# A fused layernorm, state-space and SwiGLU kernel: the half-width matmuls of all four chunks gathered in one stretch, one layernorm and four gate/up tiles moved forward

## The chip, the cores and the metric

One Trainium2 chip, one of its cores. The metric is the device time of one execution in microseconds (us); lower is better. The core works through five instruction queues, each in order: TensorE (PE, matmuls; its weight loads are shown apart as PEld), VectorE (DVE), ScalarE (ACT), GpSimd (POOL) and SyncE (SP, which only issues DMA transfers). They meet at semaphores.

## What is computed

```python
x  = A_x                                    # 1 x 2048 x 512, bf16
xn = layernorm(x)                           # over the 512 columns, eps 1e-5
# branch A: a diagonal complex recurrence along the 2048 rows
Bu[t] = xn[t] @ B_bar.T                     # complex, 512 states
h[t]  = Lam_bar * h[t-1] + Bu[t]
A = 2 * real(h @ C.T) + xn * Dskip
# branch B: SwiGLU, hidden width F = 1376
B = (silu(xn @ w_gate) * (xn @ w_up)) @ w_down
out = x + A + B
```

## The kernel before, in words

The 2048 rows are cut into four **chunks** of 512 (`CW`), c = 0 to 3, and each chunk into four row tiles of 128. Everything that a matmul reads of `xn` is its transpose `xnT`, so each chunk passes through these stages:

- **Layernorm** (`ln_rest`, L583). On DVE, for each row tile, `ln_stats` (L182: L183 and L184); then one small add (L198). POOL raises to the power -0.5 (L199), DVE forms the bias `nb` (L202), ACT writes the normalised tile `xn` (`norm_act`, L212), and SP issues a DMA transpose of it into `xnT` (L227). `ln_rest` gives two lists: the statistics (with the power), and a tail, which is `nb` and then four times "normalise one tile and transpose it". Chunk 0 has its own code at the head, and chunk 1 normalises on DVE (L207); chunks 2 and 3 do it on ACT. The buffer `xn` is single.
- **Input product of the recurrence** (`bproj_chunk`, L661): eight PSUM banks of four 128x512 matmuls (L352), copied to `u16` by ACT (L354).
- **The recurrence on DVE** (`ssm_ops`): a rotation of six wide operations (L362, L372, L376), eight scans (L394), six tiny operations that form the carry for the next chunk (L403 to L408), and a rotation back into `wt`.
- **Gate and up** (`gateup_chunk`, L669): F = 1376 is ten tiles of 128 columns and a last one of 96. A full tile is eight matmuls (L427) in two banks; ACT takes the silu of one (L441) and copies the other (L442), DVE multiplies two tiles at once (L446). The last tile (`gateup_last`, L450) packs its 96 gate columns and 32 of its 96 up columns in one bank (L453). The other 64 up columns come from `wu_last`; they fill only half of the array's columns, so two chunks share a bank, one in each half: for chunks 0 and 1 this is done when chunk 1 comes to its last tile, for chunks 2 and 3 at chunk 3's (eight matmuls each, L463). ACT copies them out (L466), and DVE multiplies (L468).
- **Output** (`out_chunk`, L675): four banks, one for each row tile, are filled by eleven matmuls from the gate/up product (L514), stay open, and are completed by eight matmuls from the recurrence (L524, which read `wt` and the matrix `CF`, made by `c_ops` from DVE L338 and ACT L335). ACT copies them out (L530) and POOL issues DMA transfers that add them to the output in memory, where `x` was copied before (L735). The last chunk goes through DVE L527.

The **order of every queue** is the order in which the program writes instructions out. PE's order is written by hand, stage after stage: gate/up of chunk 0, with its `bproj` inside; `bproj_chunk(1)`; `gateup_chunk(1)`; `bproj_chunk(2)`; `out_chunk(0)`; `gateup_chunk(2)`; `bproj_chunk(3)`; `out_chunk(1)`; `gateup_chunk(3)`; `out_chunk(2)`; `out_chunk(3)` (L725 to L753). Gate/up takes the last tile of a chunk first (L670).

The work of DVE, and of ACT and SP where an operation of the list contains it, waits in a list, `backlog`. `queue(tag, ops)` puts operations with a cost behind it, and `spread` alternates between two lists. After each piece of PE work `pump(us)` adds its time to what is owed, and writes out operations from the front as long as half of the first one's cost is owed. `need(tag)` writes out all that stands in front of the last operation with that tag. `multiply(keep)` writes out the gate/up products. Before the change, chunk 2's layernorm stands in chunk 0's recurrence and chunk 3's in chunk 1's.

PSUM is one pool of eight banks. A matmul that starts in a bank waits until ACT has copied out what was in it.

Of the kernel before, what the change touches and what calls it, by code (L numbers as in the profile page):

```python
# [11 lines left out]
BF16 = mybir.dt.bfloat16  # L12
ALU = mybir.AluOpType
# [10 lines left out]
def kernel(  # L24
# [17 lines left out]
    nc = tc.nc  # L42
    _, L, D = A_x.shape
# [3 lines left out]
    CW = 512  # L47
    HW = CW // 2
    NT = L // 128
    NCH = L // CW  # L50
    TPC = CW // 128
    KD = D // 128
    NQ = Pst // 128
    FT = (F + 127) // 128
# [4 lines left out]
    LA, LB = 32, 64  # L59
# [8 lines left out]
    up_p = ctx.enter_context(tc.tile_pool(name="up_p", bufs=4))  # L68
# [5 lines left out]
    def bank(shape=(128, CW), dtype=F32):  # L74
        return psum.tile(list(shape), dtype, name="ps")
# [11 lines left out]
    xnT = const.tile([128, KD, L], BF16, name="xnT")  # L87
# [8 lines left out]
    wu_last = const.tile([128, KD, LB], BF16, name="wu_last")  # L96
# [85 lines left out]
    def ln_stats(n):  # L182
        nc.vector.bn_stats(out=stats[:, n, 0, :], in_=xall[:, n, :])  # L183
        nc.vector.bn_aggr(out=mv[:, n, :], in_=stats[:, n, 0, :])  # L184
# [12 lines left out]
    def ln_rstd(a, b):  # L197
        nc.vector.tensor_scalar(out=ve[:, a:b], in0=mv[:, a:b, 1], scalar1=EPS, scalar2=None, op0=ALU.add)  # L198
        nc.gpsimd.tensor_tensor(out=rstd[:, a:b], in0=ve[:, a:b], in1=neg_half[:, 0:b - a], op=ALU.pow)  # L199

    def ln_nb(a, b):
        nc.vector.scalar_tensor_tensor(out=nb[:, a:b], in0=mv[:, a:b, 0], scalar=-1.0, in1=rstd[:, a:b],  # L202
                                       op0=ALU.mult, op1=ALU.mult)
# [21 lines left out]
    def xT_dma(n):  # L225
        c, i = divmod(n, TPC)
        nc.sync.dma_start_transpose(out=xnT[:, :, n * 128:(n + 1) * 128], in_=xn_tile(c)[:, i, :])  # L227
# [12 lines left out]
    V = nc.vector  # L240
# [106 lines left out]
    def bproj_tile(c, part, q):  # L347
        if c not in u_tiles:
            u_tiles[c] = ssm.tile([128, 2, NQ, CW], BF16, name="u16", bufs=2)
        ps = bank()  # L350
        for k in range(KD):
            nc.tensor.matmul(ps[:], lhsT=BT[:, part, k, q * 128:(q + 1) * 128], rhs=xnT[:, k, c * CW:(c + 1) * CW],  # L352
                             start=(k == 0), stop=(k == KD - 1))
        nc.scalar.copy(out=u_tiles[c][:, part, q, :], in_=ps[:])  # L354
# [65 lines left out]
    gu_tiles = {}  # L420
    u_pair = {}
    products = []
# [7 lines left out]
    def gu_tile(c):  # L430
        if c not in gu_tiles:
            gu_tiles[c] = gut.tile([128, FT, CW], BF16, name="guT")
        return gu_tiles[c]
# [14 lines left out]
    up_last = {}  # L448

    def gateup_last(c):  # L450
        ps = bank()
        for k in range(KD):
            nc.tensor.matmul(ps[:], lhsT=w_last[:, k, :], rhs=xnT[:, k, c * CW:(c + 1) * CW],  # L453
                             start=(k == 0), stop=(k == KD - 1))
        u = up_last[c] = up_p.tile([128, CW], BF16, name="ul", bufs=2)
        nc.scalar.activation(out=gu_tile(c)[0:LB + LA, FT - 1, :], in_=ps[0:LB + LA], func=ACT.Silu)
        nc.scalar.copy(out=u[LB:LB + LA, :], in_=ps[LB + LA:128])
        if c % 2 == 0:
            return
        ps = bank()  # L460
        for k in range(KD):
            for i in range(2):
                nc.tensor.matmul(ps[i * LB:(i + 1) * LB], lhsT=wu_last[:, k, :],  # L463
                                 rhs=xnT[:, k, (c - 1 + i) * CW:(c + i) * CW], start=(k == 0), stop=(k == KD - 1))
        for i in range(2):
            nc.scalar.copy(out=up_last[c - 1 + i][0:LB, :], in_=ps[i * LB:(i + 1) * LB])  # L466
            g, u = gu_tiles[c - 1 + i][0:LB + LA, FT - 1, :], up_last[c - 1 + i][0:LB + LA, :]
            products.append(lambda g=g, u=u: V.tensor_tensor(out=g, in0=g, in1=u, op=ALU.mult))  # L468

    def gateup_tile(c, fi):  # L470
        if fi == FT - 1:
            return gateup_last(c)
        psg = bank()
        gu_mm(psg, wg_g, c, fi, 0, CW)
        psu = bank()
        gu_mm(psu, wu_g, c, fi, 0, CW)
        gu_out(c, fi, psg, psu)
# [29 lines left out]
    def out_ffn(n):  # L507
        c, i = divmod(n, TPC)
        o_tiles[n] = []
        for lo, hi in out_blocks(n):  # L510
            o = bank((128, hi - lo))
            o_tiles[n].append(o)
            for fi in range(FT):
                nc.tensor.matmul(o[:], lhsT=gu_tiles[c][:fsz[fi], fi, i * 128:(i + 1) * 128],  # L514
                                 rhs=wd_sb[:fsz[fi], fi, lo:hi], start=(fi == 0), stop=False)
# [23 lines left out]
    def queue(tag, ops, at=None):  # L539
        ops = [[op[0], op[1], op[2] if len(op) > 2 else None, tag] for op in ops]  # L540
        if at is None:
            backlog.extend(ops)
        else:
            backlog[at:at] = ops

    def step():
        for item in backlog[0:AHEAD + 1]:
            if item[2] is not None:
                item[2]()
                item[2] = None  # L550
        cost, op, _, _ = backlog.pop(0)
        op()
        owed[0] -= cost

    def pump(us):

        owed[0] += us
        while backlog and owed[0] >= backlog[0][0] * 0.5:
            step()
        if not backlog:  # L560
            owed[0] = 0.0

    def multiply(keep):

        while len(products) > keep:
            products.pop(0)()
            owed[0] -= 0.65

    def need(tag):

        while any(item[3] == tag for item in backlog):
            step()
# [10 lines left out]
    def ln_rest(c, on_act):  # L583
        ops = [(0.7, lambda n=n: ln_stats(n)) for n in range(c * TPC, (c + 1) * TPC)]
        def fin():
            ln_rstd(c * TPC, (c + 1) * TPC)
        def nbf():
            ln_nb(c * TPC, (c + 1) * TPC)
        ops += [(0.1, fin)]
        tail = [(0.1, nbf)]  # L590
        for n in range(c * TPC, (c + 1) * TPC):
            def one(n=n):
                (norm_act if on_act else norm_dve)(n)
                xT_dma(n)
            tail.append((0.05 if on_act else 0.35, one))
        return ops, tail
# [64 lines left out]
    def bproj_chunk(c):  # L661
        need(f"ln{c}")
        for part in range(2):
            for q in range(NQ):
                bproj_tile(c, part, q)
                pump(BP)
                multiply(0 if q else 1)

    def gateup_chunk(c):  # L669
        for fi in [FT - 1, *range(FT - 1)]:  # L670
            gateup_tile(c, fi)
            pump(GU)
            multiply(1)

    def out_chunk(c):  # L675

        multiply(0)
        for n in range(c * TPC, (c + 1) * TPC):
            out_ffn(n)
            pump(FT * 0.2163)  # L680
        need(f"ssm{c}")
        need("cf")
        for n in range(c * TPC, (c + 1) * TPC):
            out_ssm(n)
            pump(2 * NQ * 0.2163)

    def spread(ops, others, tag, tag2):

        others = list(others)
        for op in ops:  # L690
            queue(tag, [op])
            if others:
                queue(tag2, [others.pop(0)])

    def queue_ssm(c):
        fwd, back = ssm_ops(c)
        queue(f"ssm{c}", fwd + back)
# [10 lines left out]
            multiply(0 if q else 1)  # L708
    fwd0, back0 = ssm_ops(0)
    stats2, norm2 = ln_rest(2, True)  # L710
    queue("ssm0", fwd0[0:2] + [(1.5, params_b)] + fwd0[2:6])
    queue("ln2", stats2)
    queue("ssm0", fwd0[6:8])
    spread(fwd0[8:] + back0, norm2, "ssm0", "ln2")
    queue("cf", c_ops())
    load_late()
    for fi in range(G0, FT):
# [6 lines left out]

    bproj_chunk(1)  # L725
    fwd1, back1 = ssm_ops(1)
    stats3, norm3 = ln_rest(3, True)
    queue("ssm1", fwd1[0:6])
    queue("ln3", stats3)
    queue("ssm1", fwd1[6:8])  # L730
    spread(fwd1[8:] + back1, norm3, "ssm1", "ln3")
    gateup_chunk(1)
    nc.gpsimd.dma_start(out=dsk_bc[:], in_=A_Dskip.partition_broadcast(128))
    bproj_chunk(2)
    nc.sync.dma_start(out=out[0, 0:(NT - TPC) * 128, :], in_=A_x[0, 0:(NT - TPC) * 128, :])  # L735
    queue_ssm(2)
    out_chunk(0)
    gateup_chunk(2)
    bproj_chunk(3)
    fwd3, back3 = ssm_ops(3)  # L740
    queue("ssm3", fwd3)
    for n in range(0, NT - TPC):
        queue("skip", [skip_op(n, False)])
        if n % TPC == TPC - 1:
            queue("skip", [(0.0, lambda c=n // TPC: skip_store(c))])
    queue("ssm3", back3)
    out_chunk(1)
    gateup_chunk(3)
    for n in range(NT - TPC, NT):
        queue("skip", [skip_op(n, True)])  # L750
    out_chunk(2)
    need("skip")
    out_chunk(3)  # L753
# [30 lines left out]
```

## Time and profile before

| | |
|---|---|
| time of three runs | 180.7, 181.02, 181.13 us (median 181.02) |
| the profiled execution's own time | 181.21 us |
| its span, first to last instruction | 179.4 us |
| PE busy | 173.4 us, 97% |
| DVE busy | 155.0 us, 86% |
| ACT busy | 104.8 us, 58% |
| start of `bproj_chunk(2)` on PE | 59.27 us |
| start of the first scan of chunk 0 on DVE | 45.84 us |

Times inside the profile count from the start of the span. The profile has a page of sums, a chain of work that ended last (followed back from the last instruction to what released it), a timeline by engine, a list of waits, and a table by stretches of time with the granted clock of TensorE. In a timeline a row is: start, duration, engine, line, operation, output and input, and how many such instructions are merged in it; in brackets, how long the engine sat idle before it and what ended that. Matmuls are pipelined: one of 512 columns is listed with 379 ns, but in a dense row they start 216 ns apart.

### The profile page before, as it was taken

To read this page: it belongs to the slowest core of one execution; us is meant where nothing else is said; L and a number is where in the kernel's file an instruction comes from. 1 tells how busy PE (TensorE), PEld (TensorE's weight loads), DVE (VectorE), ACT (ScalarE), POOL (GpSimd) and SP (SyncE) were. 2 spreads that over 40 slices of the span, in tenths; PEclk is the share of its full clock that TensorE was granted. 3 is DMA by queue.
4 is the path that set the end of the run, shared out by engine and by line. 5 is a ranking of instruction groups with operands and counts; after the bars stand their busy time and mean duration, and the time that the engine had idled before them with its cause. 6 is when DMAs were issued, how large, how long until landed. Compare 5 with 4: busy or idle time off the path is not lost.

```text
span 179.4 us, 2491 instructions
## 1 busy us (share of the span) xinstructions
PE 173.4 (97%) x908; PEld 83.4 (46%) x924; DVE 155.0 (86%) x248; ACT 104.8 (58%) x190; POOL 23.4 (13%) x30
## 2 busy tenths in 40 slices
PE   7899999999999999999999999999999999999993
PEld 2684444443444444444444444444444444444742
DVE  3649998799999999999999999999999986996033
ACT  3459956998299959022799661024866949805000
POOL 7001100000500000025400000014000004315000
PEclk9999999999999999999999999999999999999999
DMA  5999757994036600011840000007300007964512
GB/s 147 294 263 210 163 98 177 357 190 109 5 72 168 252 4 0 0 11 22 112 93 2 0 0 4 0 0 80 37 0 5 0 0 109 139 103 45 76 58 61
DMA packets 28492, 15.53 MB, mean 87 GB/s; under 512 B 18336, under 2 KB 28416, under 8 KB 28448
## 3 DMA queue, kind: packets, MB, share of 16 engines
q1 hardware_dynamic: 24592, 11.87, 28.5%
q0 software_dynamic: 3456, 3.28, 14.4%
q10 hardware_dynamic: 432, 0.23, 0.4%
q8 instruction: 7, 0.11, 0.3%
q14 instruction: 5, 0.04, 0.1%
HBM read 8.03 MB, written 5.24 MB: 74 GB/s over the span
## 4 chain that ended last, share of the span: by engine, by line
PE 93%; DMA 2%; SPq 1%; DVE 1%; issue 1%
PE ps L427 36%; PE ps L514 21%; PE ps L352 15%; PE ps L524 15%; DMA xall<-in_A_x_dram 2%; PE ps L609 2%; PE ps L453 2%; PE ps L463 1%; SPq L118 1%; DVE stats L183 0%; PE ps L219 0%; SPq L126 0%; SPq L120 0%; DVE xn L207 0%; DVE xall L527 0%
## 5 line engine op out<-in xcount | busy, mean ns | idle before, releaser
L514 PE MATMUL ps<-wd_sb,guT 128*128 128x512 bf16 (+4 forms) x195 | 38.6, 355 | 0.2
L427 PE MATMUL ps<-xnT,wg 128*128 128x512 bf16 x143 | 37.6, 379 | 0.3
L427 PE MATMUL ps<-xnT,wu 128*128 128x512 bf16 x146 | 37.5, 379 | 0.1
L394 DVE TENSOR_TENSOR_SCAN g<-r_t,car,u 128x512 bf16<-128x512 f32 x24 | 28.9, 1263 | 0.0
L524 PE MATMUL ps<-CF,wt 128*128 128x512 bf16 (+2 forms) x140 | 28.1, 355 | 0.2
L352 PE MATMUL ps<-xnT,BT 128*128 128x512 bf16 x126 | 28.2, 379 | 0.1
L514 PEld LDWEIGHTS <-guT 128*128 128x128 bf16 (+1 forms) x198 | 18.5, 98 | 19.9
L441 ACT ACTIVATE guT<-ps 128x512 bf16<-128x512 f32 x40 | 25.2, 629 | 2.5 <-PE ps L427 2.3
L442 ACT CAST u<-ps 128x512 bf16<-128x512 f32 x40 | 24.7, 618 | 2.7 <-PE ps L427 2.7
L427 PEld LDWEIGHTS <-wu 128*128 128x128 bf16 x148 | 14.5, 98 | 17.5
L427 PEld LDWEIGHTS <-wg 128*128 128x128 bf16 x148 | 14.3, 98 | 17.6 <-issue 0.8
L530 ACT CAST res<-ps 128x512 bf16<-128x512 f32 x12 | 6.8, 582 | 23.5 <-PE ps L524 23.5
L524 PEld LDWEIGHTS <-wt 128*128 128x128 bf16 x144 | 13.4, 98 | 14.3
L531 POOL DMA_DIRECT2D out_dram<-res x12 | 10.5, 1033 | 72.6 <-ACT res L530 67.5
L352 PEld LDWEIGHTS <-BT 128*128 128x128 bf16 x128 | 12.5, 98 | 15.1
L354 ACT CAST u<-ps 128x512 bf16<-128x512 f32 x32 | 17.7, 614 | 2.4 <-PE ps L352 2.2
L486 ACT ACTIVATE xr<-xall,nb,rstd 128x512 bf16<-128x512 bf16 x16 | 12.0, 808 | 8.4 <-DVE xall L492 5.9
L183 DVE BATCH_NORM_STATS2 stats<-xall 128x6 f32<-128x512 bf16 x16 | 10.7, 671 | 3.2 <-DMA xall<-in_A_x_dram 3.2
L446 DVE TENSOR_TENSOR guT<-guT,u 128x1024 bf16<-128x1024 bf16 x20 | 13.5, 679 | 0.0
L527 DVE TENSOR_TENSOR xall<-ps,xall 128x512 bf16<-128x512 f32 (+2 forms) x6 | 3.1, 514 | 9.1 <-PE ps L524 9.1
L199 POOL TENSOR_TENSOR rstd<-ve,neg_half 128x4 f32<-128x4 f32 x3 | 5.3, 1751 | 43.6 <-DVE ve L198 43.6
L362 DVE TENSOR_TENSOR pm<-u,c 128x2048 bf16<-128x2048 bf16 x8 | 9.8, 1221 | 1.2 <-ACT c L279 1.1
(101 smaller groups left out, 169.0 us busy)
## 6 DMA issues: line engine op xcount, KB each, us to landing
out_dram<-in_A_x_dram SPq DMA_DIRECT2D x1, 1536.0 KB, 8.7
out_dram<-res POOLq DMA_DIRECT2D x12, 128.0 KB, 3.2
out_dram<-xall POOLq DMA_DIRECT2D x3, 512.0 KB, 5.7
wd_sb<-in_B_w_down_dram SPq DMA_DIRECT2D x1, 1280.0 KB, 10.1
xall<-in_A_x_dram SPq DMA_DIRECT2D x1, 1024.0 KB, 5.9
wg<-in_B_w_gate_dram SPq DMA_DIRECT2D x1, 512.0 KB, 6.1
wu<-in_B_w_up_dram SPq DMA_DIRECT2D x1, 512.0 KB, 7.1
xall<-in_A_x_dram SPq DMA_DIRECT2D x1, 512.0 KB, 7.9
```

Source lines behind the costliest of these rows:

```text
L183: nc.vector.bn_stats(out=stats[:, n, 0, :], in_=xall[:, n, :])
L352: nc.tensor.matmul(ps[:], lhsT=BT[:, part, k, q * 128:(q + 1) * 128], rhs=xnT[:, k, c * CW:(c + 1) * CW], start=(k == 0), stop=(k == KD - 1))
L354: nc.scalar.copy(out=u_tiles[c][:, part, q, :], in_=ps[:])
L394: V.tensor_tensor_scan(out=g()[:, part, q, :], data0=r_t[:, q:q + 1].to_broadcast([128, CW]), data1=u_tiles[c][:, part, q, :], initial=ini ...
L427: nc.tensor.matmul(ps[:fs, lo:hi], lhsT=wslice(groups, fi, k), rhs=xnT[:, k, c * CW + lo:c * CW + hi], start=(k == 0), stop=(k == KD - 1))
L441: nc.scalar.activation(out=guT[:fs, fi, :], in_=psg[:fs], func=ACT.Silu)
L442: nc.scalar.copy(out=u_pair[c][:fs, fi % 2, :], in_=psu[:fs])
L446: products.append(lambda: V.tensor_tensor(out=g, in0=g, in1=u, op=ALU.mult))
L486: nc.scalar.activation(out=box["xr"][:], in_=xall[:, n, :], func=ACT.Identity, scale=rstd[:, n:n + 1], bias=nb[:, n:n + 1])
L514: nc.tensor.matmul(o[:], lhsT=gu_tiles[c][:fsz[fi], fi, i * 128:(i + 1) * 128], rhs=wd_sb[:fsz[fi], fi, lo:hi], start=(fi == 0), stop=False)
L524: nc.tensor.matmul(o[:], lhsT=w_tiles[c][:, part, q, i * 128:(i + 1) * 128], rhs=CF[:, part, q, lo:hi], start=False, stop=(part == 1 and q ...
L531: nc.gpsimd.dma_start(out=out_v[:, n, lo:hi], in_=res[:, lo:hi], accum_op=ALU.add)
```

## The change

Four things are done.

1. The half-width matmuls of all four chunks stand together, in a new function `up_halves`, between `gateup_chunk(1)` and `bproj_chunk(2)`: eight for chunks 0 and 1, then eight for chunks 2 and 3. The copies by ACT follow, and the last-tile products of chunks 0 and 1 are queued there; chunks 2 and 3 queue theirs in `gateup_last`. The buffers `ul` are four in place of two.
2. So that `xnT` of chunk 3 is there, its layernorm is moved from chunk 1's recurrence into chunk 0's, behind chunk 2's: on DVE, six scans of chunk 0 come before chunk 3's statistics, then two scans and the carry, then chunk 3's `nb`, and the four pairs of normalisation and transpose alternate with the rotation back. `need("ln2")` and `need("ln3")` stand in front of `up_halves`.
3. Chunk 2's tiles 0 to 3 of gate and up are computed inside `out_chunk(0)`, between the two groups of its matmuls.
4. Chunk 2's last tile comes at the end of its gate/up stage, as number 10 of `range(4, FT)`.

```diff
-        u = up_last[c] = up_p.tile([128, CW], BF16, name="ul", bufs=2)
+        u = last_up(c)
         nc.scalar.activation(out=gu_tile(c)[0:LB + LA, FT - 1, :], in_=ps[0:LB + LA], func=ACT.Silu)
         nc.scalar.copy(out=u[LB:LB + LA, :], in_=ps[LB + LA:128])
-        if c % 2 == 0:
-            return
-        ps = bank()
-        for k in range(KD):
+        if c >= 2:
+            last_product(c)
+
+    def last_up(c):
+        if c not in up_last:
+            up_last[c] = up_p.tile([128, CW], BF16, name="ul", bufs=NCH)
+        return up_last[c]
+
+    def last_product(c):
+        g, u = gu_tiles[c][0:LB + LA, FT - 1, :], last_up(c)[0:LB + LA, :]
+        products.append(lambda: V.tensor_tensor(out=g, in0=g, in1=u, op=ALU.mult))
+
+    def up_halves():
+        pair = [bank() for _ in range(0, NCH, 2)]
+        for c0, ps in zip(range(0, NCH, 2), pair):
+            for k in range(KD):
+                for i in range(2):
+                    nc.tensor.matmul(ps[i * LB:(i + 1) * LB], lhsT=wu_last[:, k, :],
+                                     rhs=xnT[:, k, (c0 + i) * CW:(c0 + i + 1) * CW],
+                                     start=(k == 0), stop=(k == KD - 1))
+        for c0, ps in zip(range(0, NCH, 2), pair):
             for i in range(2):
-                nc.tensor.matmul(ps[i * LB:(i + 1) * LB], lhsT=wu_last[:, k, :],
-                                 rhs=xnT[:, k, (c - 1 + i) * CW:(c + i) * CW], start=(k == 0), stop=(k == KD - 1))
-        for i in range(2):
-            nc.scalar.copy(out=up_last[c - 1 + i][0:LB, :], in_=ps[i * LB:(i + 1) * LB])
-            g, u = gu_tiles[c - 1 + i][0:LB + LA, FT - 1, :], up_last[c - 1 + i][0:LB + LA, :]
-            products.append(lambda g=g, u=u: V.tensor_tensor(out=g, in0=g, in1=u, op=ALU.mult))
+                nc.scalar.copy(out=last_up(c0 + i)[0:LB, :], in_=ps[i * LB:(i + 1) * LB])
+        for c in range(2):
+            last_product(c)
...
-    def gateup_chunk(c):
-        for fi in [FT - 1, *range(FT - 1)]:
+    def gateup_chunk(c, tiles=(FT - 1, *range(FT - 1))):
+        for fi in tiles:
...
-    def out_chunk(c):
+    def out_chunk(c, between=None):
 
         multiply(0)
         for n in range(c * TPC, (c + 1) * TPC):
             out_ffn(n)
             pump(FT * 0.2163)
+        if between:
+            between()
         need(f"ssm{c}")
...
     stats2, norm2 = ln_rest(2, True)
+    stats3, norm3 = ln_rest(3, True)
     queue("ssm0", fwd0[0:2] + [(1.5, params_b)] + fwd0[2:6])
     queue("ln2", stats2)
     queue("ssm0", fwd0[6:8])
-    spread(fwd0[8:] + back0, norm2, "ssm0", "ln2")
+    spread(fwd0[8:12], norm2, "ssm0", "ln2")
+    queue("ln2", norm2[4:])
+    queue("ln3", stats3)
+    queue("ssm0", fwd0[12:14])
+    spread(fwd0[14:] + back0, norm3, "ssm0", "ln3")
...
     fwd1, back1 = ssm_ops(1)
-    stats3, norm3 = ln_rest(3, True)
-    queue("ssm1", fwd1[0:6])
-    queue("ln3", stats3)
-    queue("ssm1", fwd1[6:8])
-    spread(fwd1[8:] + back1, norm3, "ssm1", "ln3")
+    queue("ssm1", fwd1 + back1)
     gateup_chunk(1)
     nc.gpsimd.dma_start(out=dsk_bc[:], in_=A_Dskip.partition_broadcast(128))
+    need("ln2")
+    need("ln3")
+    up_halves()
+    pump(2 * KD * 0.2163)
     bproj_chunk(2)
...
-    out_chunk(0)
-    gateup_chunk(2)
+    out_chunk(0, lambda: gateup_chunk(2, range(0, 4)))
+    gateup_chunk(2, range(4, FT))
     bproj_chunk(3)
```

## The prediction

> **What bounds the kernel now.** The page's sums and its chain by engine say TensorE:
>
> ```profile
> PE 173.4 (97%) x908; PEld 83.4 (46%) x924; DVE 155.0 (86%) x248; ACT 104.8 (58%) x190; POOL 23.4 (13%) x30
> ...
> PE 93%; DMA 2%; SPq 1%; DVE 1%; issue 1%
> ```
>
> A busy PE could still be a slow PE, so the next view is the table by stretches, across the place of the change and from there to the last matmul (columns: stretch, length, busy time and count of PE, PEld, DVE, ACT and POOL, then the granted clock of TensorE):
>
> ```profile
> 40.00:59.27 19.27, 19.16 (x92) 8.50 (x93) 19.06 (x33) 14.86 (x29) 2.44 (x2) 1.00 0.41 102
> 59.27:176.40 117.13, 116.53 (x572) 54.80 (x581) 104.17 (x135) 60.91 (x105) 16.31 (x16) 1.00 0.26 42
> ...
> 178.00:179.40 1.40, 0.00 (x0) 0.00 (x0) 0.00 (x0) 0.00 (x0) 0.00 (x0) 0.89 0.02 6
> ```
>
> PE has no hole of note, at full clock. A matmul stream without holes can't win time by order, and a hole put into it is lost whole, since no later hole takes it up. But DVE is as full as PE from 40 to 59 us (19.06 of 19.27). So the question for a step moved forward on DVE is when it is done, and the timeline of DVE tells the price of each operation there (start, duration, line, count):
>
> ```profile
> 45.84 2.33 DVE L394 TENSOR_TENSOR_SCAN g<-r_t,u 128x512 bf16<-128x512 f32 x2
> 48.08 0.40 DVE L468 TENSOR_TENSOR guT<-guT,ul 96x512 bf16<-96x512 bf16 x1
> 48.40 1.21 DVE L394 TENSOR_TENSOR_SCAN g<-r_t,u 128x512 bf16<-128x512 f32 x1
> 49.53 0.13 DVE L202 SCALAR_TENSOR_TENSOR nb<-mv,rstd 128x4 f32<-128x4 f32 x1
> ```
>
> From start to start: a scan 1.12 us (two from 45.84 to 48.08), a last-tile product 0.32, `nb` 0.06. By the same rows elsewhere: four row tiles' statistics with the add 3.40 (42.44 to 45.84), a two-tile product 0.60 (57.79 to 58.40), the carry 0.54 (56.12 to 56.66).
>
> Behind `nb` comes ACT, and this is how its timeline looks now for chunk 2:
>
> ```profile
> 49.70 0.81 ACT L212 ACTIVATE xn<-xall,nb,rstd 128x512 bf16<-128x512 bf16 x1 [3.46 <-DVE nb L202]
> 50.42 0.58 ACT L441 ACTIVATE guT<-ps 128x512 bf16<-128x512 f32 x1
> 50.90 0.57 ACT L442 CAST u<-ps 128x512 bf16<-128x512 f32 x1
> 51.36 0.82 ACT L212 ACTIVATE xn<-xall,nb,rstd 128x512 bf16<-128x512 bf16 x1
> ```
>
> ACT starts 0.17 us behind `nb`, a normalisation takes 0.72 us, and one with two evictions behind it 1.66. ACT stood 3.46 us for `nb`, and PE did not: the eight banks gave it that much room. Chunk 2's `xnT` is first read at 59.27, long after; there the wait was free.
>
> **The change part by part.** All positions below follow the order in which the changed program writes out each queue.
>
> *The gathered stretch.* Now eight half-width matmuls, in pairs, stand at 41.00 behind four that start from 40.05, and full ones follow at 41.99:
>
> ```profile
> 40.05 1.03 PE L453 MATMUL ps<-xnT,w_last 128*128 128x512 bf16 x4
> 41.00 1.05 PE L463 MATMUL ps<-xnT,wu_last 128*64 128x512 bf16 x8
> 41.99 1.04 PE L427 MATMUL ps<-xnT,wg 128*128 128x512 bf16 x4
> ```
>
> Entry to exit is 1.94 us for what is eight slots of 0.216 (four, and four pairs), 1.73: 0.2 us for going into this shape and out. Four matmuls of it are as long in one stretch as in two, so merging saves 0.2 us, once, if the stretch isn't broken.
>
> *When chunk 3's `xnT` lands.* On DVE nothing changes up to the first scan at 45.84. Then: three scans, `nb` of chunk 2, three scans, three of chunk 3's statistics, a product (L446), the fourth, the small add, two scans, a product, the carry, `nb` of chunk 3. Eight scans are 9.00, `nb` 0.06, statistics 3.40, two products 1.20, carry 0.54; sum 14.20, so `nb` of chunk 3 starts at 60.04. POOL's power (1.85 us) is behind the add at 56.6 and done before. The last-tile products that stood there now come later.
>
> ACT can't normalise ahead of it, and its queue is in order. The four normalisations of chunk 3 stand behind tile 7's evictions, behind tile 8's, and two behind tile 9's: 60.21, 61.87, 63.53, 64.25. SP issues each transpose 0.84 us behind its normalisation's start (50.54 behind 49.70), and one after the other at 1.29 us (four in 5.16):
>
> ```profile
> 21.95 5.16 SPq L227 DMA_TRANSPOSE xnT<-xn  x4
> ...
> xnT<-xn SPq DMA_TRANSPOSE x12, 2.4
> ```
>
> So the third is issued at 64.37, the fourth at 65.66, and it lands 2.4 later: **68.06**. The second half of the stretch reads it.
>
> *When PE is there.* `gateup_chunk(1)` starts 1.08 us earlier, at 40.91, and its ten tiles of 1.73 would end at 58.18. Two small stalls come in: both pairs of chunk 2's normalisations stand together, so tile 6 waits for the bank of tile 2 (ACT 49.39, two times 0.72, one silu: 0.2 us) and tile 7 for that of tile 3 (two more normalisations: 0.7 us). PE ends tile 9 at 59.1 and the first half at 60.1. Then it waits from 60.1 to about 68.1, **8.0 us**; the small stalls, and the saving inside the stretch, are swallowed. `bproj_chunk(2)` follows 0.98 us behind, at 69.1, in place of 59.27; and 0.98 us of L463 is gone from `gateup_chunk(3)`. The shift is 68.1 − 59.27 = **8.8 us**.
>
> *The clock behind the hole.* No row of before has a hole of 8 us inside the stream, so I bound it. The program's first ten matmuls, behind an idle PE, start at 1.23 and are followed at 5.25 by others:
>
> ```profile
> 1.23 4.19 PE L581 MATMUL ps<-junk 128*128 128x512 bf16 x10 [1.23 <-DVE eps_t L164]
> 5.25 0.28 PE L219 MATMUL ps<-ident,xn 128*128 128x128 bf16 x2
> ```
>
> That is 4.02 us where the stream needs ten times 0.216, 2.16: 1.9 us more. And when PE stops at 176.4, the granted clock of the last 1.4 us is 0.89 in the mean; if it went from 1 to one half, it did so at 179.1, 2.7 us after the last matmul. The ends are thus 0 (clock kept) and 1.9 (or half as much again, 2.9, if the wake-up takes longer). I take 1.9, because the hole is far longer than 2.7 us and the start is the only row in which PE comes out of a long wait. The Trainium skill, "TensorE: Matmul & The Clock Gate", section "What's actually happening", has a rule that speaks against this change: an idle window of some 3.4 us puts the array to half rate, and about 3.4 us of busy time lift it. By its figures the loss would be an estimated 1.7 us and the time 191.7; the head and the tail of this trace agree with it, and no row shows it in mid-program.
>
> *What else moves.* SP: the copy of `x` to the output, behind the transposes, is issued at 67 in place of 56.80 and takes 8.7 us; the first addition to it came at 78.50 and will come after 96. POOL: the load of `dsk_bc` stands behind chunk 3's power, at 59 in place of 47.82; it is used in the last third. Both at nothing. Chunk 2's four tiles inside chunk 0's output: the same matmuls in another order. Four banks stay open and four rotate, so a bank comes round after two tiles, 3.45 us, while ACT needs 1.0 us a tile: nothing, unless ACT is late. What is late next is `CF`: its eight ACT parts now stand behind the copies of the second half, so from 71; with eight bproj evictions between them (0.7 and 0.6 us each) they end about 82. `out_ssm` of chunk 0 needs it after bproj (6.9), out_ffn (9.5) and the four tiles (6.9), at 94: 12 us of cover, which the moved tiles give. Chunk 1's scans free `u16` for `bproj_chunk(3)` at 100, PE is there at 112. DVE loses about 6 us waiting for ACT, PE moves by more, so the later stages gain room. All at nothing.
>
> Sum: 8.8 + 1.9 = 10.7 us on the profiled execution's own 181.21 (its span 179.4 and 1.8 around it): **191.9 us**. That execution lies 0.2 us above the median of the three runs, 181.02; I don't correct for it.
>
> **The rivals.**
>
> *The hole without the clock.* PE comes out at full rate: 181.2 + 8.8 = 190.0. For it: no row shows a slow matmul after 5.25. Against: the half clock in the tail. 0.13.
>
> *The transposes are in time, and one entry and exit is saved:* 181.2 − 0.2 = 181.0, not slower. It decides at one point: from `nb` to the last landing is 68.06 − 60.04 = 8.02 us, so for a landing by 59.2 the `nb` of chunk 3 must stand at 51.2. DVE has 14.2 us of work ahead of it from 45.84 on, and would have to be 9 us quicker; every term of that sum is measured. 0.02.
>
> *A second wait.* `CF` or chunk 1's `wt` isn't ready when PE comes to `out_chunk(0)`'s second part, or four banks do not cover ACT. It starts to cost when `CF` is later than 94 against 82; ACT late by 14 us more would add 2: 193.9 or more. Against: the cover above. 0.05.
>
> *The layernorm is not the last to come:* the changed order does less than it says. It would need the six-scan place to be late only for the statistics, with the normalisations spread over empty ACT time, and half of the wait: 4.4 + 1.9, 187.5. ACT's two last normalisations stand together and behind evictions that are done by 63.5, so only about 1 us could be won. 0.04.
>
> **How the numbers follow.** Forecast 0.76, and the rivals as given. A measurement of this kernel can tell about 0.3%, 0.5 us, from no change. The range: the hole within 0.5 us either way (DVE's sum of 14.2 us, one landing), clock from 0 to 2.9. Low 189.5 is the second case less 0.5; high 193.4 is 181.2 + 8.8 + 2.9 + 0.5. The cases left out are 0.11 and the edges some 0.06. The case in time is 0.02, half of it for a gain that shows: faster 0.01, same 0.01, slower 0.98, the rest.
>
> **What would show it.** In the changed profile: a PE idle of about 8 us released by the transposes, in the middle of the half-width stretch; ACT idle for `nb` twice, about 4.2 and 2.1 us; `nb` of chunk 3 at 60.0; after the hole some 10 matmul slots at 427 ns and a granted clock below 1 in that slice alone; `bproj_chunk(2)` at 69 to 70; PE dense from there to the end, at the old 117 us less 1 plus the slow slots. Wrong would be: PE reaching the second half and finding `xnT` there (`nb` before 51), a second hole, or full rate behind the first.

## The result, and the profile after

| | before | after |
|---|---|---|
| median of the runs | 181.07 us (180.7 to 181.45, 4 runs) | 192.39 us (191.56 to 192.7, 4 runs) |
| ratio to before | | 1.0624, 95% interval 1.0601 to 1.0646 |
| span of the profiled execution | 179.4 us | 190.6 us |
| mean granted clock of TensorE | 0.999 | 0.973 |

The change makes the kernel 6.2% slower; 191.9 was forecast. In the page's sums and its chain by engine, TensorE is no longer the whole story:

```profile
PE 176.4 (93%) x908; PEld 84.4 (44%) x924; DVE 155.9 (82%) x248; ACT 106.3 (56%) x190; POOL 23.3 (12%) x30
...
PE 64%; DVE 24%; ACT 4%; DMA 4%; issue 2%; SPq 1%; DVEq 0%
```

The instruction counts are the same, PE's 908 among them. Yet PE is busy 3 us longer with them (some matmuls are slower), and the span is 11.2 us longer (there is a hole too). The chain, followed back from the end, now leaves PE and runs through DVE and ACT: what ends last in the first part of the program is no longer matmuls. The timeline of PE shows where (columns as before: start, duration, and in brackets the idle time and its releaser):

```profile
58.98 1.27 PE L475 MATMUL ps<-xnT,wu_last 128*64 128x512 bf16 x9
68.03 1.86 PE L475 MATMUL ps<-xnT,wu_last 128*64 128x512 bf16 x7 [7.79 <-DMA xnT<-xn]
69.82 7.50 PE L352 MATMUL ps<-xnT,BT 128*128 128x512 bf16 x26
```

One matmul of the second half got through at 59.86, since it reads chunk 2; the next reads chunk 3 and waits until 68.03 for a transpose. The stages of the chain that released it, on DVE, ACT and SP:

```profile
59.83 0.16 DVE L202 SCALAR_TENSOR_TENSOR nb<-mv,rstd 128x4 f32<-128x4 f32 x1
```

```profile
49.29 1.52 ACT L212 ACTIVATE xn<-xall,nb,rstd 128x512 bf16<-128x512 bf16 x2 [4.25 <-DVE nb L202]
...
60.08 0.81 ACT L212 ACTIVATE xn<-xall,nb,rstd 128x512 bf16<-128x512 bf16 x1 [2.05 <-issue]
...
63.39 1.54 ACT L212 ACTIVATE xn<-xall,nb,rstd 128x512 bf16<-128x512 bf16 x2
```

```profile
62.58 4.17 SPq L227 DMA_TRANSPOSE xnT<-xn  x3
```

The two idle times in brackets are the two waits of ACT for `nb`, of chunk 2 and of chunk 3 (the second one's releaser, DVE, isn't named, but `nb` ends 0.1 us before). The last two normalisations stand together behind tile 9's evictions. The last of the three transposes in SP's row is issued at 65.54. And the table by stretches, with the granted clock in the third column from the right:

```profile
58.98:60.08 1.10, 1.10 (x10) 0.47 (x9) 1.10 (x9) 0.01 (x1) 0.14 (x1) 1.00 0.09 22
60.08:63.09 3.01, 0.16 (x1) 0.00 (x0) 3.01 (x4) 3.01 (x6) 0.00 (x0) 1.00 0.41 79
63.09:68.03 4.94, 0.00 (x1) 0.13 (x2) 4.87 (x5) 2.88 (x5) 0.00 (x0) 0.50 0.43 83
68.03:73.33 5.30, 5.30 (x16) 1.88 (x16) 2.59 (x6) 2.99 (x5) 0.00 (x0) 0.50 0.79 297
73.33:187.40 114.07, 113.48 (x556) 53.68 (x565) 93.70 (x116) 55.34 (x93) 14.36 (x15) 1.00 0.24 31
```

PE idle from 60.08; the clock at one half from 63.09, 3.0 us later; 16 listed matmuls in the 5.30 us behind the hole; and from 73.33 to the last matmul PE is as dense as before. One hole and its echo in the clock: PE's other waits in that profile are 0.5 us or less, but for 1.2 us at the program's start, which stood there before.

### The profile page after: what moved, and what is told of

It is laid out like the page before. It is cut to its first block, busy times and chain, and to the rows that moved or that the text cites. A ratio compares the mean times of both kernels' runs of the same rounds, so it can differ in the third digit from the quotient of the medians.

```text
span 190.6 us, 2486 instructions
## 1 busy us (share of the span) xinstructions
PE 176.4 (93%) x908; PEld 84.4 (44%) x924; DVE 155.9 (82%) x248; ACT 106.3 (56%) x190; POOL 23.3 (12%) x30
## 4 chain that ended last, share of the span: by engine, by line
PE 64%; DVE 24%; ACT 4%; DMA 4%; issue 2%; SPq 1%; DVEq 0%
PE ps L528 20%; PE ps L427 18%; PE ps L538 14%; PE ps L352 8%; DVE stats L183 4%; DVE g L394 4%; DVE pm L275 3%; DVE pm L362 2%; DMA xall<-in_A_x_dram 2%; DVE guT L446 2%; ACT xn L212 2%; DVE pm L274 1%; DMA xnT<-xn 1%; DVE mv L184 1%; PE ps L475 1%
## 5 line engine op out<-in xcount | busy, mean ns | idle before, releaser
L441 ACT ACTIVATE guT<-ps 128x512 bf16<-128x512 f32 x40 | 24.4, 610 | 11.4 <-PE ps L427 11.4
L352 PE MATMUL ps<-xnT,BT 128*128 128x512 bf16 x125 | 29.8, 396 | 0.2
L442 ACT CAST u<-ps 128x512 bf16<-128x512 f32 x40 | 24.0, 599 | 4.3 <-PE ps L427 4.3
L545 POOL DMA_DIRECT2D out_dram<-res x12 | 10.5, 1041 | 81.6 <-ACT res L544 81.6
L354 ACT CAST u<-ps 128x512 bf16<-128x512 f32 x32 | 17.6, 598 | 3.2 <-PE ps L352 3.0
L541 DVE TENSOR_TENSOR xall<-ps,xall 128x512 bf16<-128x512 f32 (+2 forms) x6 | 3.1, 514 | 11.3 <-PE ps L538 11.2
L338 DVE SCALAR_TENSOR_TENSOR CF<-CT,nc2im,cm 128x512 bf16<-128x512 bf16 x8 | 5.8, 750 | 7.3 <-ACT cm L335 7.3
```

What stands on the lines that cost most here:

```text
L441: nc.scalar.activation(out=guT[:fs, fi, :], in_=psg[:fs], func=ACT.Silu)
L442: nc.scalar.copy(out=u_pair[c][:fs, fi % 2, :], in_=psu[:fs])
L545: nc.gpsimd.dma_start(out=out_v[:, n, lo:hi], in_=res[:, lo:hi], accum_op=ALU.add)
```

## The experiments

**One part alone: chunk 2's tiles inside chunk 0's output.** From the kernel before:

```diff
-    out_chunk(0)
-    gateup_chunk(2)
+    out_chunk(0, lambda: gateup_chunk(2, range(0, 4)))
+    gateup_chunk(2, range(4, FT))
```

> The kernel before with one part of the change alone: chunk 2's tiles 0 to 3 inside chunk 0's output, its last tile at the end. My theory (the whole loss is the wait for chunk 3's transposes and the clock behind it): the same matmuls in another order, four rotating banks are enough: 181.1 us, within 0.3%. Rival (four banks do not cover ACT's evictions): each of four tiles stalls by 0.2 to 0.5 us, 182 to 183 us, with a wait of PE for ACT inside that stage.

Measured: 180.91 us, ratio 1.0 (0.9984 to 1.0015). PE is dense through the four tiles, which rotate in four banks:

```profile
75.38 1.03 PE L427 MATMUL ps<-xnT,wg 128*128 128x512 bf16 x4
...
81.42 1.03 PE L427 MATMUL ps<-xnT,wu 128*128 128x512 bf16 x4
82.28 7.07 PE L524 MATMUL ps<-CF,wt 128*128 128x512 bf16 x32
```

Eight banks' worth from 75.38 to 82.28 is 0.863 us each, four times 0.216: nothing is lost. This part is innocent.

**The same part undone in the changed kernel.**

```diff
-    out_chunk(0, lambda: gateup_chunk(2, range(0, 4)))
-    gateup_chunk(2, range(4, FT))
+    out_chunk(0)
+    gateup_chunk(2)
```

> The changed kernel with that part undone: chunk 2's gate and up behind the whole of chunk 0's output. My theory: CF is ready at about 82 us and PE asks for it about 88.2 in place of 95, so nothing waits: 192.4 us as the changed kernel. Rival (the moved tiles were the cover that CF needs): a second hole, 193 us or more, with PE waiting for DVE L338.

Measured: 191.94 us, ratio 1.0609 (1.0582 to 1.0635), which overlaps the changed kernel's. On DVE the last of `CF` is written from about 81.2, and PE reads it at 87.29 without a wait, the one hole being the known one:

```profile
67.55 1.86 PE L475 MATMUL ps<-xnT,wu_last 128*64 128x512 bf16 x7 [7.78 <-DMA xnT<-xn]
69.34 8.59 PE L352 MATMUL ps<-xnT,BT 128*128 128x512 bf16 x32
77.77 9.68 PE L528 MATMUL ps<-wd_sb,guT 128*128 128x512 bf16 x44
87.29 7.07 PE L538 MATMUL ps<-CF,wt 128*128 128x512 bf16 x32
```

The moved tiles were not needed as cover.

**The early layernorm kept, its reader moved back.** From the changed kernel; the second half of the stretch goes behind the first matmuls of chunk 0's output:

```diff
-    up_halves()
-    pump(2 * KD * 0.2163)
+    up_halves([0])
+    pump(KD * 0.2163)
     bproj_chunk(2)
...
-    out_chunk(0, lambda: gateup_chunk(2, range(0, 4)))
+    def between0():
+        up_halves([2])
+        gateup_chunk(2, range(0, 4))
+    out_chunk(0, between0)
```

> The changed kernel with its stretch cut in two: chunks 0 and 1 stay where they are, chunks 2 and 3 are read behind the first matmuls of chunk 0's output, at about 76 us, when the last transpose has landed for 8 us. Chunk 3's layernorm stays early. My theory (the loss comes from reading xnT too early, not from doing the layernorm early): no hole, full clock; what stays is the 0.7 us of PE stalls at gate/up tiles 6 and 7 of chunk 1, and up to 0.3 us for the first last-tile product: 181.7 to 182.2 us. Rival (the early layernorm itself costs, through CF, wt or the evictions behind the normalisations): 184 us or more.

Measured: 181.77 us, ratio 1.0051 (1.0032 to 1.0069), clock 1.0. That gives back 10.5 of the 11.3 us. So the layernorm's early place costs 0.84 us at most; that PE asks for its result at 60 us costs the rest. The 0.84 us are what the small stalls cost, 0.17 and 0.65:

```profile
50.89 1.02 PE L427 MATMUL ps<-xnT,wg 128*128 128x512 bf16 x4
51.75 1.03 PE L427 MATMUL ps<-xnT,wu 128*128 128x512 bf16 x4
53.26 1.02 PE L427 MATMUL ps<-xnT,wg 128*128 128x512 bf16 x4 [0.48 <-ACT guT L441]
```

Four matmuls are 0.86 us. The group before these started at 49.86, so 50.89 is 0.17 late; from 51.75 the next would start at 52.61 and starts at 53.26, 0.65 late (the bracket counts from the modelled end of the last matmul, 0.17 behind its slot). Both wait for a bank.

**And two of chunk 2's normalisations apart.** From the split run, a statistics operation of chunk 3 is put in front of the third, two in front of the fourth:

```diff
-    spread(fwd0[8:12], norm2, "ssm0", "ln2")
-    queue("ln2", norm2[4:])
-    queue("ln3", stats3)
+    spread(fwd0[8:11], norm2[0:3], "ssm0", "ln2")
+    queue("ssm0", fwd0[11:12])
+    queue("ln3", stats3[0:1])
+    queue("ln2", norm2[3:4])
+    queue("ln3", stats3[1:3])
+    queue("ln2", norm2[4:])
+    queue("ln3", stats3[3:])
```

> As the run with the split stretch, and chunk 2's third and fourth normalisations stand apart on ACT, with a statistics operation of chunk 3 in between, so that two tiles' evictions lie between them. My theory: the PE stall at tile 7 goes (0.5 us), the 0.2 us at tile 6 stays: 181.2 to 181.7 us, some 0.5 under the split run. Rival: the stall only moves to a later tile, same as the split run.

Measured: 181.78 us, ratio 1.0051 (1.0032 to 1.007): a miss, and the rival's result. One tile's evictions now lie between the two normalisations, not two tiles'. The stall at tile 7 is gone, and one as long has come in `bproj_chunk(2)`:

```profile
58.02 1.05 PE L475 MATMUL ps<-xnT,wu_last 128*64 128x512 bf16 x8
59.01 6.22 PE L352 MATMUL ps<-xnT,BT 128*128 128x512 bf16 x28
65.74 1.02 PE L352 MATMUL ps<-xnT,BT 128*128 128x512 bf16 x4 [0.52 <-ACT ul L480]
```

PE came earlier to a bank that ACT copies out only behind chunk 3's normalisations, and ACT's place there is set by `nb` on DVE, which had not moved. Here a stall taken out ahead of another in-order wait was paid there.

**The hole filled.** From the changed kernel, with matmuls on zeros into the bank that the second half overwrites, 36, 28 and 18 of them:

```diff
         for c0, ps in zip(range(0, NCH, 2), pair):
+            for _ in range(36 if c0 else 0):
+                nc.tensor.matmul(ps[:], lhsT=junk[:, 0:128], rhs=junk[:], start=True, stop=True)
```

> The changed kernel with 36 needless matmuls of 128x512 on zeros in the hole, written to the bank that the second half overwrites: 7.8 us of the 8.0. They change no result; they keep PE busy. My theory (the slow matmuls behind the hole are the clock's answer to an idle PE): clock 1.00 throughout, the hole's 8.8 us stay, the 2.5 us behind it go: 190.0 us. Rival (the matmuls behind the hole are slow for another reason, such as the transfers or weight loads that start there): 192.4 us as the changed kernel.

> The same with 28: PE idles for the last 1.9 us. If about 3 us of idle time are needed, the clock stays at 1.00: 190.0 us. If any hole of some us lowers it: 191 us or more.

> The same with 18: PE idles for the last 4.0 us of the hole. In the traces so far the clock fell 2.7 and 3.0 us after the last matmul. If it is idle time of about 3 us that counts, it falls here too: 191.6 to 192.5 us. If half a hole is short enough to keep it: 190.0 us.

Measured: 189.84 us (ratio 1.0477, 1.0448 to 1.0507) with 36; 189.72 (1.048, 1.0452 to 1.0507) with 28; 191.26 (1.0556, 1.0523 to 1.0589) with 18. With 36 matmuls that nobody needs the kernel is 2.6 us faster than without them, so that much of the loss is the clock's. With 28, PE idles 1.7 us, and with 18, 3.9; the stretches around the end of the hole:

```profile
66.20:67.88 1.68, 0.16 (x2) 0.11 (x2) 1.65 (x2) 0.00 (x0) 0.00 (x0) 1.00 0.40 78
67.88:73.30 5.42, 5.42 (x28) 2.46 (x28) 3.00 (x6) 4.33 (x8) 0.00 (x0) 1.00 0.79 290
```

```profile
64.20:66.45 2.25, 0.18 (x1) 0.00 (x0) 2.25 (x3) 1.80 (x4) 0.00 (x0) 1.00 0.41 81
66.45:68.05 1.60, 0.00 (x1) 0.13 (x1) 1.57 (x2) 0.00 (x0) 0.00 (x0) 0.50 0.41 82
68.05:73.28 5.23, 5.23 (x16) 1.82 (x16) 2.52 (x6) 2.99 (x5) 0.00 (x0) 0.50 0.80 301
```

In 5.4 us behind the hole, 28 matmuls in the first, 16 in 5.2 us in the second, at the same share of the transfers (0.79 and 0.80). The transfers don't make them slow.

The profile with 18 is of the slowest of its six runs, 192.39 us at a mean clock of 0.982. One more took 192.12 at that clock, and four took 190.94 to 191.36 at 0.991. So the clock fell in all six, as expected, but in four it cost only 1.2 to 1.6 us over the run with 28, and the median lies below the expected 191.6 to 192.5.

**`nb` of chunk 3 earlier.** From the changed kernel, another order on DVE:

```diff
-    spread(fwd0[8:12], norm2, "ssm0", "ln2")
-    queue("ln2", norm2[4:])
-    queue("ln3", stats3)
-    queue("ssm0", fwd0[12:14])
-    spread(fwd0[14:] + back0, norm3, "ssm0", "ln3")
+    spread(fwd0[8:9], norm2[0:1], "ssm0", "ln2")
+    queue("ln3", stats3)
+    spread(fwd0[9:13], norm2[1:], "ssm0", "ln2")
+    queue("ln3", norm3[0:1])
+    queue("ssm0", fwd0[13:14])
+    spread(fwd0[14:] + back0, norm3[1:], "ssm0", "ln3")
```

> The changed kernel with another order on DVE: chunk 3's statistics ahead of five of the eight scans, its nb ahead of the last scan and the carry. By the measured durations nb stands at 57.6 us in place of 59.83, the last normalisation at 62.75, the last landing at 66.0 in place of 68.03. My theory (the chain DVE nb, ACT, SP, landing sets the end of the hole, one for one): 2.0 us less, 190.4 us, give or take 0.9 for the clock. Rival (the SP queue or the transfers set the landing): no change, 192.4 us.

Measured: 192.65 us, ratio 1.0635 (1.0604 to 1.0667): a miss, no gain. On DVE the chain moved as worked out: `nb` stands at 57.14, 11.9 us behind the first scan (45.23; this trace runs 0.5 us ahead of the changed kernel's), in place of 14.1. Two links behind it did not follow. The first is ACT:

```profile
57.99 0.81 ACT L212 ACTIVATE xn<-xall,nb,rstd 128x512 bf16<-128x512 bf16 x1 [2.42 <-DMA xnT<-xn]
```

What releases ACT is no longer `nb` but chunk 2's last transpose, which reads the single buffer `xn` until 57.88; that is some 0.7 us behind the place that follows from `nb`. In the changed kernel the same transpose had landed at 56.51, ahead of `nb`. So the last normalisation stands at 62.98 and its transpose is issued at 63.85, in place of 64.1 and 65.54. The second link is the landing: PE goes on at 68.22. In the list of transfers from 65 to 68.3 that transpose takes 4.3 us to land, not 2.4, and these are around it:

```profile
q1 hardware_dynamic: 560, 0.92, 88.7%
q8 instruction: 1, 0.02, 2.5%
...
out_dram<-in_A_x_dram SPq DMA_DIRECT2D x1, 1536.0 KB, 7.1
xnT<-xn SPq DMA_TRANSPOSE x1, 4.3
```

Each transpose leaves 16 marks of its end in the trace, as many as there are DMA engines. Fifteen came by 66.25; the sixteenth came at 68.17. One packet of the instruction queue, 16 KB, ran from 65.76 to 67.08, and the last small packets of the transfer stand right at its end, at 67.06 and 67.08. The copy of `x` to the output, issued just behind the transposes, was then running with packets of 48 KB and some 2 us, so either could be the cause.

**The same with that copy out of the way.**

```diff
     for part, src in enumerate((A_C_re, A_C_im)):
         for q in range(NQ):
             nc.sync.dma_start_transpose(out=CT[:, part, q, :], in_=src[:, q * 128:(q + 1) * 128])
+    nc.sync.dma_start(out=out[0, 0:(NT - TPC) * 128, :], in_=A_x[0, 0:(NT - TPC) * 128, :])
...
     bproj_chunk(2)
-    nc.sync.dma_start(out=out[0, 0:(NT - TPC) * 128, :], in_=A_x[0, 0:(NT - TPC) * 128, :])
```

> The run with nb early, which gained nothing: 15 of the 16 marks of its last transpose came by 66.25, as worked out, and the last one at 68.17, while the copy of x to the output, issued right behind at 65.09 with its 48 KB packets of 2 us, was running. Here that copy stands ahead of chunk 2's transposes in SP's queue, behind the transposes of C, at about 44 us. Theory (one engine's last mark stood behind a packet of the copy): the last landing at 66.2, PE goes on there, 2.0 us less, 190.7 us, give or take 0.9 for the clock. Rival (the last transpose is slow for another reason): PE goes on at 68.2 again, 192.6 us.

Measured: 191.34 us, ratio 1.0579 (1.0542 to 1.0617), 1.3 us less than with the copy behind and 1.05 less than the changed kernel. The last transpose lands in 2.9 us, and PE goes on at 67.33, not at 66.2:

```profile
xnT<-xn SPq DMA_TRANSPOSE x1, 2.9
```

```profile
L227 SPq DMA_TRANSPOSE xnT<-xn x1: 1842/1842/1842, 64.3 to 64.3; - x1
```

But the theory does not hold. The instruction packet ran here too, from 64.54 to 65.76, and met the transpose before the last: 15 of that one's marks came by 65.07, the sixteenth at 66.81, 1.74 us behind, with no copy running. With the copy it was 1.92. So a mark about as late comes without the copy, and a part of the copy in it is not shown. Of the 96 transposes of chunks 2 and 3 in the twelve profiles these two alone have their last mark more than 0.25 us behind the fifteenth. The last transpose here has its 16 marks together, 67.15 to 67.28; it is 0.5 late, and SP took 1.84 us to issue it, where others take 1.2.

So the packet is what both late marks have in common; no run takes it away, so that it is the cause is argued and not shown. In the profiles PE goes on 0.9 us earlier than with the copy behind, and the clock stays low behind the hole for 2.95 us in place of 4.35. That clock is this one run's (190.57 us, 0.982); the three others, at 0.970 to 0.973, took 191.03 to 191.7. What sets the packet's time, and why SP took longer, stays open. ACT waited for the buffer `xn` here as well: `nb` at 57.47, its first normalisation at 58.49.

**The price of a stretch.** From the kernel before, each pair of half-width matmuls behind one full-width one, which makes eight stretches of two:

```diff
+        halves = bank() if c % 2 else None
         for k in range(KD):
             nc.tensor.matmul(ps[:], lhsT=w_last[:, k, :], rhs=xnT[:, k, c * CW:(c + 1) * CW],
                              start=(k == 0), stop=(k == KD - 1))
+            for i in range(2 if c % 2 else 0):
+                nc.tensor.matmul(halves[i * LB:(i + 1) * LB], lhsT=wu_last[:, k, :],
+                                 rhs=xnT[:, k, (c - 1 + i) * CW:(c + i) * CW], start=(k == 0), stop=(k == KD - 1))
```

> The kernel before with the half-width matmuls cut up: each pair stands behind one of the four full-width matmuls of the odd chunk's last tile, so there are eight stretches in place of two, and the work is the same. My theory (0.2 us for each going in and out, the one thing that gathering could save): six more, 1.3 us, 182.4 us. Rival (paid once, or only a matter of the records): 181.1 us.

Measured: 182.31 us against 180.89 of the kernel before beside it, ratio 1.0073 (1.0056 to 1.0089). 1.42 us for six more stretches: 0.24 each. In the timeline a full-width matmul and a pair are two slots, 0.43 us, and take 0.66:

```profile
40.23 0.41 PE L457 MATMUL ps<-xnT,wu_last 128*64 128x512 bf16 x2
40.57 0.39 PE L454 MATMUL ps<-xnT,w_last 128*128 128x512 bf16 x1
40.89 0.41 PE L457 MATMUL ps<-xnT,wu_last 128*64 128x512 bf16 x2
```

The Trainium skill, "TensorEngine Tiling (Array Packing)", section "Key Properties", says that a change of tiling mode drains the array, without a price. In this case going in and out costs 0.24 us. That is also all that having one stretch less can save in this kernel, 0.13% of its time, less than its measurement can tell. A version that gathers them and waits for nothing was therefore not tried.

## Why the prediction was right

*PE-bound, so a hole is lost whole.* Right. Behind 73.33 nothing took up any of it, and the hole and its echo give the whole difference: 68.03 − 59.27 = 8.76 us for the hole, 2.5 for the clock, sum 11.3; the spans differ by 11.2.

*The chain to the last landing.* Right, each link within 0.25 us: `nb` at 60.04 forecast, 59.83 measured; the last two normalisations 63.53 and 64.25, measured from 63.39 on; the last transpose issued 65.66, 65.54; PE goes on 68.06, 68.03. The sum of 14.2 us on DVE was taken from the neighbours' rows in the trace of before; the terms of that sum came out within 0.05 us each in their new places. The run with the reader moved back shows that it is the reading. That the hole's end follows `nb` one for one is not shown: with `nb` 2.2 us earlier, counted from the first scan, PE went on 0.7 us later in one run and 0.5 earlier in the other, since the single buffer `xn` and the landing ended last there. The forecast's chain has no term for that buffer, and takes the landing at 2.4 us always. In the changed kernel neither counted: the buffer was free at 56.51, and the instruction packet came at 67.85, just as the marks came in (67.84 to 67.98). The second was luck that the forecast didn't know of.

*The small stalls.* 0.9 forecast in sum, 0.8 measured, and, as said, swallowed by the hole; they show where the hole is gone.

*The clock.* The mechanism was right, and the size was the mis-sized term of the sum: 1.9 us taken from the head of the program, 2.5 measured here (the tenth matmul of `bproj_chunk(2)` starts at 73.49; at full rate behind 68.03 it would be 0.98 and nine slots of 0.216 later, 70.95), 2.6 by the filled run. That was inside the bounds of 0 and 2.9. At the head the slow matmuls lasted 4.0 us; behind this hole they lasted 5.3. (The table by stretches gives 1.00 for the head, but the clock's first entry in that trace stands at 5.0 us, where the slow matmuls end; ahead of it nothing is recorded.) The rule of the Trainium skill ("TensorE: Matmul & The Clock Gate", "What's actually happening": some 3.4 us idle to fall, 3.4 busy to rise, in windows that run by themselves) has the right shape, and the 1.7 us estimated from it was low for the profiled execution. The traces agree with free-running windows: the stretch at half rate, hole and all, is 10.24 us here and with `nb` early, 6.83 with 18 fillers and with the copy early, that is three and two times 3.41, wherever PE came back in it. The stretches at full clock ahead of the fall are multiples too: 58.03 us here (17 times), 61.44 with 18 fillers (18 times), 174.08 before (51 times). By that reading the loss depends on where the hole falls in a window, and the runs fit it: the one run of the changed kernel with a mean clock of 0.982 took 191.56 us, 1.7 over the filled run, and the three others lie 2.5 to 2.9 over it.

*The rest at nothing.* Right: the moved tiles alone 1.0, without them nothing saved or lost; `CF`, `wt`, the copy to the output and `dsk_bc` made no wait.

*The rivals.* The hole without the clock is what the filled kernel shows, 189.84 (190.0 was worked out). Transposes in time would have needed `nb` 9 us earlier; the 2.2 us by which two runs had it earlier became 1.05 us of time in one and none in the other. A second wait isn't there. Nor did the layernorm come in time for half of the wait: the hole is 7.95 us long, as forecast (8.0).

## What to carry to other kernels

When one engine is full, ask of a moved step not what it costs but when its result lands at the first reader: sum the in-order queues and the single buffers that it goes through, engine by engine, and compare with the reader's slot. A hole in this full matmul stream cost its length, and more for the clock: about 2.5 us behind 8 us of idle time, 1.2 to 2.7 behind 3.9 us, nothing behind 1.7 us. Where a hole can't be avoided, needless matmuls in it gave that part back. And before making room for a saving, price it by multiplying it: eight stretches told in one run that two could never be worth more than half a microsecond, and that gathering them saves 0.24.

## What the runs showed of the hardware that was not expected

- PE went on when the last of a transpose's 16 marks was in. In the two profiles in which a 16 KB packet of the instruction queue (1.2 and 1.3 us) began 0.4 us ahead of the first mark, one of the 16 was 1.7 and 1.9 us late, once without and once with the copy of `x` beside it. In the changed kernel the packet began with the marks, and none was late.
- The clock fell 2.3, 2.6, 2.7, 3.0, 3.6 and 4.4 us behind the last matmul (18 fillers, the moved part undone, the end of before, the changed kernel, `nb` early, copy early) and not within 1.7. It came back 5.3, 5.2, 4.35 and 2.95 us behind the first matmul of the four holes (changed, 18 fillers, `nb` early, copy early). The runs' times go with that phase: of the changed kernel's, one with a mean clock of 0.982 took 191.56 us, three with 0.971 to 0.973 took 192.38 to 192.7.
- Six goings in and out of the half-width shape cost 1.42 us, 0.24 each.
